# A long-convolution layer and a linear-memory attention layer in one kernel: two PSUM banks per product, Q's feature map in one piece, the last projection in five banks, a new written-out order

## The chip, the cores and the metric

The kernel runs on one core of a Trainium2 chip. The core has a matrix engine (TensorE, PE in the profile; its weight loads are PEld), a vector engine (VectorE, DVE), a scalar engine (ScalarE, ACT), GpSimd (POOL) and a queue engine (SyncE, SP) that here does nothing but issue transfers. Matrix products land in PSUM, eight banks of 512 fp32 columns on 128 partitions; DVE and ACT read them out into SBUF. The metric is the device time of one execution in microseconds; less is better. Three runs of the kernel before gave 274.84, 274.92 and 275.57 us.

## The reference

Two independent layers share the output, 640 columns each. With S = 2048 positions and D = 640 channels:

```python
# layer A: short causal filter on k, gate with v, long causal convolution, gate with q
kv = k_shift * v                                  # k_shift: 4 taps per channel
y = irfft(rfft(pad(kv)) * rfft(pad(ssm_k)))[:S]   # length 2S, per channel
a = q * (y + kv * ssm_D)

# layer B: 32 heads of 20, four segments of 512 positions
phi = lambda t: where(t > 0, t + 1.0, exp(t))
for s in range(4):
    p = softmax(qs @ ks.T * scale + mask)         # causal, inside the segment
    a_mem = (phi(qs) @ M) / (phi(qs) @ z + 1e-6)  # memory of earlier segments
    o = g * a_mem + (1 - g) * (p @ vs)
    M, z = M + phi(ks).T @ vs, z + phi(ks).sum()
b = concat(o) @ wo
return concatenate([a, b], axis=-1)
```

## The kernel before

**Layer A** (`conv`, line 428) runs over five slices `dp` of 128 channels. For each slice: the convolution's filter is brought in with positions on partitions (`load_filter`, 437; for slice 0 on PE as four groups `kt`, else by transposing transfers through DRAM); k is loaded transposed; the short filter is four PE groups `ks`, each one bank of 512 columns, and DVE multiplies each by v in place in `vt` (512). `spectrum` (515) transforms `vt` (X) and the filter (K) in eight PE groups F of 512 columns, read out by `evict` into a buffer F, followed by sums and differences on DVE (`B`). `product` (548) multiplies the spectra in sixteen DVE operations (`P1` to `YB`). `inverse` (584) goes back in four groups `I` of 512 columns, each multiplied by q on DVE into `qd` (597), and stores them; slice 4 stores each quarter on its own.

**Layer B** has eight units u: four segments s, each in two halves of 16 heads. `project` (636) takes four tiles of 128 positions: K, Q and V are three PE groups of 320 columns (`P`, `V`), read out by `evict`; K and Q of a tile are transposed by one transfer on SP into KQT (667). The feature map phi (668 to 680) is made for K in one piece of four tiles, and for Q in two pieces of two tiles; a piece is one exponential on ACT, two operations on DVE, and for Q a transposing transfer on SP into PqT. It is made for K in segments 0 to 2 and for Q in segments 1 to 3. Then comes an upper bound for the softmax (`kam`, `bound`: absolute values `qabs` of the transposed Q on DVE, a PE group `bd`, its read-out bT, four small `rows` transfers on SP into KQT). `attend` (722) makes ten times two blocks of scores on PE, each pair of banks read by one exponential of 1024 columns on ACT into a buffer ET, and then the values (`O`) with the memory's part in a second bank, a reciprocal and two products on DVE (`N`). `project_out` (815) transposes o (segments 0 to 2 by transfers on SP, segment 3 on PE as five groups `ot`) and multiplies it by wo: per segment four tiles, each two groups of 320 columns, and one store per tile. In segment 3 each group's matmuls are issued in three parts, by the channels of o that they need.

**What sets the order.** All operations are recorded first (`Recorder`, 105), each with the engine's queue that it goes to; a matmul group recorded under `rec.one()` is one operation, or one part of it. `ORDER` (866) is a packed list, a permutation of all operations, in which they are then issued (`issue`, 247; each instruction of the program carries line 256). Each engine works off its own share of that list strictly in that order, and so does SP with the transfers. `BASE` (889) gives each PSUM group its first bank. `EVICT` (863) has one digit per read-out: 1 sends it to DVE, 0 to ACT (`evict`, 387). Nothing is decided while the kernel runs. The first twenty PE groups (`warm`) multiply zeros while the first transfers come in.

The names in the profile are those of the buffers: `ET<-ps` is an exponential of scores, `F<-ps` the read-out of a spectrum, `KQ<-ps` and `Va<-ps` read-outs of K, Q, V, `vt<-ps,vt` the product of the short filter, `pq<-ps,pq` that of the inverse, `outb<-ps` and (in the last segment, where PP serves as a buffer) `PP<-ps` the read-outs of the last projection, `KQT<-KQ` and `PqT<-PP` the transposing transfers, `xT<-in_B_x` x's.

Of the kernel before, what the change touches and what calls it, by code (L numbers as in the profile page):

```python
# [16 lines left out]
ALU = mybir.AluOpType  # L17
# [4 lines left out]
S = 2048; D = 640  # L22
# [242 lines left out]
class Layer:  # L265
# [162 lines left out]
    def conv(self, dp):  # L428
# [31 lines left out]
        def short_filter():  # L460
# [33 lines left out]
            for b in range(4):  # L494
                key("ks", b)
                g = self.group(1, "ks")
                ps = g.ap[:, 0, :]
# [14 lines left out]
                V.tensor_tensor(out=vt[:, b], in0=ps.rearrange("p (c d) -> p c d", d=128), in1=vt[:, b], op=ALU.mult, grp=g)  # L512
# [71 lines left out]
        def inverse(U):  # L584
# [51 lines left out]
    def project(self, u):  # L636
# [5 lines left out]
        for t in range(4):  # L642
            tok = slice(128 * t, 128 * t + 128)
            rec.key = ("P", u, t)
            for i0 in range(0, 2, KQW):
                g = self.group(KQW, "kq")
                for i in range(KQW):
                    with rec.one():
                        for cc in range(5):
                            nc.tensor.matmul(g.ap[:, i, 0:320], lhsT=xT[:, cc, tok], rhs=self.wqkv[:, cc, half, i0 + i, :], start=(cc == 0), stop=(cc == 4), grp=g)  # L650
                self.evict(KQ[:, t, i0:i0 + KQW, :, 0:DH], g.ap[:, :, 0:320].rearrange("p i (h d) -> p i h d", d=DH), g)
            rec.key = ("V", u, t)
            g = self.group(1, "v")
            with rec.one():
                for cc in range(5):
                    nc.tensor.matmul(g.ap[:, 0, 0:320], lhsT=xT[:, cc, tok], rhs=self.wqkv[:, cc, half, 2, :], start=(cc == 0), stop=(cc == 4), grp=g)
            self.evict(Va[:, t, :, 0:DH], g.ap[:, 0, 0:320].rearrange("p (h d) -> p h d", d=DH), g)
# [10 lines left out]
            for i, n in ((0, 4), (1, 2)):  # L668
# [146 lines left out]
    def project_out(self, s):  # L815
# [13 lines left out]
        else:  # L829
            oTv = self.ring("xT", None)[:].rearrange("p c q -> p (c q)").rearrange("p (t c q) -> p t c q", t=4, c=5)  # L830
            for t in range(0, 4, 2):
                rec.key = ("oT", s, t)
                nc.sync.dma_start_transpose(out=oTv[:, t:t + 2].rearrange("p t c q -> p (t c) q"), in_=self.o_s[s][:, t:t + 2])
        for t in range(4):
# [32 lines left out]
c-jrrgMttW5Czb=cV=>JwrjI(+um&3wry{=YqM?Jwr#$5KH?;hgpx=SOA<*c$t1Z1N(ymFDKR9bq>|JUAo(PXq?L4%UNVSCM#(S5rG&(nOj1M&N>M2#1thZ+l7x&T#UzwOl)_R{vPd?GD$yjTv=&M_Ru  # L867
o89mX@*-N1{t2Mv-!&Vp2)cGmt4+Mq){M36cs@RjNxireH0}!<rIV^0I}rlxosSYDjI##|%ux29lBaS%3|tvec1!l9;)qoph2aQdc@ieJRM$5?k6xRtYPOq`f3zW692(>@3OIQQAr&c9R^;#a_}>nn)M
vA=xDh2T5~jCVeC~3$vf3W>?7}xuv_LWf2aRb<$e~$W-=~o)XM35>EO{JQ*lOS&TzuIE!<wWa1c(U|yNV5=_dmoW;pZ!`U3l;j&svaSn&c6lP{JR^W6FV;K&WJTgKmu_7yT97}TsOLC-yNEMEfF*2T2x
kkoHZI<OG87D7Um*u!omdkiq$So4Ytul!dqz*@N0XNHfnJA-KiyNdS=Q5m*mTEjCqqvCkSe-{ib&}NJVQIqfI+HtOmo(*kHsfM8=M;%6dt|q?py@uDEJtOk?3H?K%l%TGD<p>Ql<+cL>NAWsV0#8jJI2  # L870
(8T*7Xgz($-S0Xj{Va;AjUmh8?0a!`7(F}KM?u96wDjLW%FRx+A)W^~;yj<A?5D>zHKa0BCNS3*~@6+?JT;^|zWu4Ws?*VgR7dD4+<*`EU#Swo`}7t09=hvRZVF3Cv=g(#Xpd$JdANfO=2Q*uu3$Yn{Y
YdDan<)WOI-VBdq+J}R9L)Nh`T?2I!Bk664s&}OyZ^{x0gE)Fc&d7c)l;j#pugO(8z!Z9rgPBU#^SUgO)H;L-br0uDB2A-b<(@2%`|?2cavOW=KJMT{+05;Xj6S+dq9CnC(8uyfw(ufD>sF@I2<WTbG_
gj+C0=Gf-N}eLOuK7T9O7<9!f@Ti6FkYoTq;i`gQnC$dX7hUl;@dVfm1xqCz4Scg9t!0Twr`;(q}SQk1;x)%W-Db1ZavE5(7<ei!pJBu{5iW*DQL5u`ohk%59!yY`wx)l3gcgHqD`NahGpoq+a7yc2UJ
WUT0EF*Vl5NH`!GmGdAAJ5KV|1d@oP<MV>Ma9`GR(p&9aNGQ>jxO^kPvUmx)qCu)Cv&Lk+PA7y|VKFAAxma*Crlk}4m)=`>U$LVP8p;Ps%{F1zy96j}$<kUi%M~iC<{FYvt675hz15rx9OKEM7AM#VmX
h|)ilXZ%wKsvl)Q7x;}G!vSmnC3w_&47xU9vP7unUPDMXeFJYsZd$-Vx|t%@;X#=V76A#Y{-IKsGvD9Mzf=;25VL{*4$`?CR$DB=yGkKt<h8)X+xc>f7LCN{nNTyPgiI@%+m$h2J>~H#<Kiqi&<I#X|P
D^YdEW+1yNJ~$Y1GzAdPL2Ervyq`Y422`dgz|OnbwBQeD-SX(B6(@U~bxqK>A8;3JEo0cxw+TdvkW8p%HK9h>PAU8`%f4~ihbB3N^6p~cWrY46z=ZFQZt(gYUIT5EB%)A-h2*XsuDXx)&|x}$@3vJh?a
f43bqv6aL|?WCKu6GmBB>w*$UV%rqf8KZ5dMzvB{s@ruRB3ftNrO|D-Ho^{#W_xtACbQBQfUZbx4Y60ZXb;<u&wR~+2(+HIPs^a2ZPnwN+74)U`@*C)*izU@J*Z`ILWfvNJET2O73EP5?d`1g#9{4V=d
# [87 lines left out]
```

## Time and profile before

| | us |
|---|---|
| three runs, median | 274.92 |
| the profiled execution | 274.51 |
| its span, first to last instruction | 272.7 |
| PE busy | 259.2 |
| DVE busy | 252.3 |
| ACT busy | 244.4 |
| POOL busy | 6.9 |

The busy time of an engine is the time in which at least one of its instructions was under way; neighbouring instructions overlap, so the durations in a group's row add up to more. The clock of TensorE was granted in full throughout. A group's row shows engine, operation, output and inputs, shapes, count, then busy time and mean ns of one, then the idle time of the engine just before them with what ended it. In the timeline the columns are start, length, engine, and the operation; `x3` are three in a row. SPq marks the issuing of a transfer on SP. Matmul ends are modelled, and PE's busy time takes in waits between them.

### The profile page before, as it was taken

To read this page: it belongs to the slowest core of one execution; us is meant where nothing else is said; L and a number is where in the kernel's file an instruction comes from. 1 tells how busy PE (TensorE), PEld (TensorE's weight loads), DVE (VectorE), ACT (ScalarE), POOL (GpSimd) and SP (SyncE) were. 2 spreads that over 40 slices of the span, in tenths; PEclk is the share of its full clock that TensorE was granted. 3 is DMA by queue.
4 is the path that set the end of the run, shared out by engine and by line. 5 is a ranking of instruction groups with operands and counts; after the bars stand their busy time and mean duration, and the time that the engine had idled before them with its cause. 6 is when DMAs were issued, how large, how long until landed. Compare 5 with 4: busy or idle time off the path is not lost.

```text
span 272.7 us, 10081 instructions
## 1 busy us (share of the span) xinstructions
PE 259.2 (95%) x4337; PEld 193.8 (71%) x4339; DVE 252.3 (93%) x426; ACT 244.4 (90%) x378; POOL 6.9 (3%) x18
## 2 busy tenths in 40 slices
PE   8999999999999999869999999999999999898994
PEld 3888677768678678747777687777776876675883
DVE  0799999999999999969999999999998999999972
ACT  1374699999999999969999999999999999999953
POOL 9000000000000000000000000000000000000000
PEclk9999999999999999999999999999999999999999
DMA  6999889999779899997999899873996047581333
GB/s 202 296 240 175 203 184 193 262 233 176 138 160 167 192 223 169 119 249 173 174 160 211 186 223 148 172 118 79 157 182 152 29 84 146 122 138 45 64 105 118
DMA packets 131196, 44.79 MB, mean 164 GB/s; under 512 B 121563, under 2 KB 128736, under 8 KB 131024
## 3 DMA queue, kind: packets, MB, share of 16 engines
q1 hardware_dynamic: 130992, 43.96, 82.0%
q8 instruction: 34, 0.56, 0.9%
q0 software_dynamic: 160, 0.20, 0.2%
q14 instruction: 10, 0.08, 0.2%
HBM read 14.12 MB, written 7.34 MB: 79 GB/s over the span
## 4 chain that ended last, share of the span: by engine, by line
PE 53%; ACT 24%; DVE 11%; issue 4%; DMA 4%; SPq 3%; DVEq 0%; ACTq 0%
PE ps L256 53%; ACT ET L256 16%; ACT F L256 4%; SPq L256 3%; DVE pq L256 2%; ACT KQ L256 2%; DMA out_dram<-pq 2%; DVE Y L256 2%; DMA out_dram<-outb 1%; DVE o L256 1%; ACT Va L256 1%; ACT PP L256 1%; DVE Xh L256 1%; DVE Kh L256 1%; DVE F L256 1%
## 5 line engine op out<-in xcount | busy, mean ns | idle before, releaser
L256 ACT ACTIVATE ET<-ps 128x1024 bf16<-128x1024 f32 x160 | 159.0, 1072 | 0.9 <-PE ps L256 0.6
L256 PEld LDWEIGHTS <-xT 128*128 128x128 bf16 x640 | 58.8, 98 | 28.2 <-issue 6.5
L256 PE MATMUL ps<-wqkv,xT 128*128 128x320 bf16 x480 | 76.9, 299 | 1.9 <-DMA xT<-in_B_x_dram 1.0
L256 PE MATMUL ps<-Va,ET 128*128 128x21 bf16 x1280 | 42.8, 172 | 1.0 <-ACT KQ L256 0.6
L256 PEld LDWEIGHTS <-ET 128*128 128x128 bf16 x1280 | 40.0, 96 | 3.6 <-issue 2.4
L256 ACT CAST F<-ps 128x512 bf16<-128x512 f32 x71 | 39.8, 644 | 1.4 <-PE ps L256 1.4
L256 PE MATMUL ps<-KQT 32*128 32x128 bf16 (+2 forms) x896 | 35.2, 239 | 0.8 <-ACT ET L256 0.4
L256 PEld LDWEIGHTS <-Wf 128*128 128x128 bf16 x320 | 28.8, 97 | 5.8 <-issue 1.7
L256 ACT CAST KQ<-ps 128x320 bf16<-128x320 f32 x61 | 27.1, 477 | 5.9 <-PE ps L256 5.9
L256 PE MATMUL ps<-wo,xT 128*128 128x320 bf16 x160 | 25.8, 299 | 0.6 <-ACT ET L256 0.5
L256 PEld LDWEIGHTS <-KQT 32*128 32x128 bf16 x896 | 16.2, 92 | 11.3 <-issue 10.4
L256 PE MATMUL ps<-vt,Wf 128*128 128x256 bf16 x160 | 22.1, 273 | 0.3 <-ACT ET L256 0.3
L256 PE MATMUL ps<-kT,Wf 128*128 128x256 bf16 x160 | 21.3, 272 | 0.0
L256 PE MATMUL ps<-Y,Wi 128*128 128x256 bf16 x160 | 20.5, 273 | 0.2
L256 DVE TENSOR_TENSOR o<-ps,rr 128x640 bf16<-128x640 f32 x24 | 19.5, 812 | 0.2
L256 PE MATMUL ps<-Mbd,PqT 128*128 128x84 bf16 x96 | 18.4, 202 | 0.9 <-ACT ET L256 0.9
L256 DVE TENSOR_TENSOR Y<-Y,pq 128x2048 bf16<-128x2048 bf16 (+1 forms) x20 | 18.7, 935 | 0.0
L256 ACT ACTIVATE PP<-KQ 128x640 bf16<-128x640 bf16 (+1 forms) x18 | 17.5, 971 | 0.8 <-DVE KQ L256 0.7
L256 DVE TENSOR_TENSOR pq<-Xh,Kh 128x2048 bf16<-128x2048 bf16 x15 | 18.2, 1211 | 0.0
L256 PEld LDWEIGHTS <-Wi 128*128 128x128 bf16 x160 | 14.8, 98 | 3.4 <-issue 1.3
L256 PE MATMUL ps<-skd,kr 128*128 128x128 bf16 (+4 forms) x114 | 16.0, 255 | 0.4 <-ACT ET L256 0.3
L256 PEld LDWEIGHTS <-kr 128*128 128x128 bf16 x116 | 14.5, 148 | 2.3 <-issue 0.6
(90 smaller groups left out, 355.8 us busy)
## 6 DMA issues: line engine op xcount, KB each, us to landing
vt<-in_A_v_dram SPq DMA_DIRECT2D x10, 256.0 KB
pq<-in_A_q_dram SPq DMA_DIRECT2D x10, 256.0 KB
out_dram<-outb SPq DMA_DIRECT2D x13, 160.0 KB
turned<-kT SPq DMA_DIRECT2D x4, 512.0 KB
kT<-turned SPq DMA_DIRECT2D x8, 256.0 KB
out_dram<-pq SPq DMA_DIRECT2D x8, 256.0 KB
kb<-kr SPq DMA_DIRECT2D x6, 256.0 KB
Wf<-c_wf SPq DMA_DIRECT2D x4, 256.0 KB
```

The source lines that it names most:

```text
L256: f(*[fix(a) for a in args], **{k: fix(v) for k, v in kw.items()})
```

## The change

- **Two banks per operation in layer A.** Two neighbouring groups of the short filter (`KSW = 2`) take two banks side by side, and one DVE operation of 1024 columns multiplies both by v. The same for the inverse and q (`IW = 2`). The matmuls are the same. Slice 4's stores are issued in two sets of four.
- **Q's feature map in one piece** (`QN = 4`): four tiles at once: one exponential, two DVE operations and one transfer per unit in place of two each.
- **The last projection in five banks** (`WP = 1`): in segment 3, each of the four tiles has one group of 512 columns; the remaining 128 columns of the four tiles share a fifth group. Five read-outs of 512 columns in place of eight of 320, and five stores: four of 128 rows of 1024 bytes, one of 512 rows of 256 bytes.
- **A new order, new banks, new shares**: `ORDER` and `BASE` are replaced, and `EVICT` has 227 digits with 31 ones in place of 230 with 33. The program has 1476 operations in place of 1531, and 180 transfers on SP in place of 185.
- A joint group for K, Q and V is written but not used (`KQV = 0`).

```diff
-                g = self.group(1, "ks")
-                ps = g.ap[:, 0, :]
+                if b % KSW == 0:
+                    g = self.group(KSW, "ks")
+                ps = g.ap[:, b % KSW, :]
...
-                V.tensor_tensor(out=vt[:, b], in0=ps.rearrange("p (c d) -> p c d", d=128), in1=vt[:, b], op=ALU.mult, grp=g)
+                if b % KSW == KSW - 1:
+                    some = vt[:, b + 1 - KSW:b + 1].rearrange("p b c d -> p b (c d)")
+                    V.tensor_tensor(out=some, in0=g.ap, in1=some, op=ALU.mult, grp=g)
...
-                g = self.group(1, "I")
-                pyv = g.ap[:, 0, :].rearrange("p (a h d) -> p a h d", a=2, h=2)
+                if c % IW == 0:
+                    g = self.group(IW, "I")
+                pyv = g.ap[:, c % IW, :].rearrange("p (a h d) -> p a h d", a=2, h=2)
...
-                V.tensor_tensor(out=qd[:, :, c, :], in0=g.ap[:, 0, :].rearrange("p (b d) -> p b d", d=128), in1=qd[:, :, c, :], op=ALU.mult, grp=g)
+                if c % IW < IW - 1:
+                    continue
+                some = qd[:, :, c + 1 - IW:c + 1, :]
+                V.tensor_tensor(out=some, in0=g.ap.rearrange("p c (b d) -> p b c d", d=128), in1=some, op=ALU.mult, grp=g)
...
-                        nc.sync.dma_start(out=rows.rearrange("(p h c) d -> p c h d", h=2, c=4)[:, c], in_=qd[:, 2 * a:2 * a + 2, c, :])
+                        for n in range(c + 1 - IW, c + 1):
+                            nc.sync.dma_start(out=rows.rearrange("(p h c) d -> p c h d", h=2, c=4)[:, n], in_=qd[:, 2 * a:2 * a + 2, n, :])
...
-            for i, n in ((0, 4), (1, 2)):
+            for i, n in ((0, 4), (1, QN)):
...
+        if last and WP:
+            rem = self.group(1, "w")
+            rest = self.ring("outb", [128, 2, 320], n=2)[:].rearrange("p i j -> p (i j)")[:, 0:512]
+            for t in range(4):
+                g = self.group(1, "w")
+                for part in ((0, 1, 2), (3,), (4,)):
+                    with rec.one():
+                        for cc in part:
+                            nc.tensor.matmul(g.ap[:, 0, :], lhsT=oTv[:, t, cc, :], rhs=self.wo[:, cc, 0:512], start=(cc == 0), stop=(cc == 4), grp=g)
+                self.evict(spare[:, 512 * t:512 * t + 512], g.ap[:, 0, :], g)
+                nc.sync.dma_start(out=self.out[L * s + 128 * t:L * s + 128 * t + 128, D:D + 512], in_=spare[:, 512 * t:512 * t + 512])
...
+            for part in ((0, 1, 2), (3,), (4,)):
+                with rec.one():
+                    for t in range(4):
+                        for cc in part:
+                            nc.tensor.matmul(rem.ap[:, 0, 128 * t:128 * t + 128], lhsT=oTv[:, t, cc, :], rhs=self.wo[:, cc, 512:640], start=(cc == 0 and t == 0), stop=(cc == 4), grp=rem, skip_group_check=True)
+            self.evict(rest, rem.ap[:, 0, :], rem)
+            nc.sync.dma_start(out=self.out[L * s:L * s + 512, D + 512:2 * D].rearrange("(t p) j -> p t j", p=128), in_=rest.rearrange("p (t j) -> p t j", t=4))
+            return
...
+WP = 1
+KSW, IW = 2, 2
+KQV, QN = 0, 4
...
-EVICT = ("01011011111000100000001000000000000000000000000000000000000001000000000000001010000000101100000100000000000000000001000000000000000000000000"
-         "000000000100001110000000000000000000000000010001000000000000010100100000100001010001100100")
+EVICT = ("01010010000000010000001000000000000000000000000000000000000000000000000000000000000000011000110100100000000000000000001100000000000000000000"
+         "000000000010111010000000100000000100000000100001001001010000000100100000110100000000100")
```

More of the change, by code (lines that the diff above doesn't have):

```diff
@@ L644, in project @@
             rec.key = ("P", u, t)
-            for i0 in range(0, 2, KQW):
-                g = self.group(KQW, "kq")
-                for i in range(KQW):
+            if KQV:
+                g = self.group(2, "kqv")
+                w = self.wqkv[:, :, half].rearrange("p c i j -> p c (i j)")
+                for b in range(2):
                     with rec.one():
                         for cc in range(5):
-                            nc.tensor.matmul(g.ap[:, i, 0:320], lhsT=xT[:, cc, tok], rhs=self.wqkv[:, cc, half, i0 + i, :], start=(cc == 0), stop=(cc == 4), grp=g)
-                self.evict(KQ[:, t, i0:i0 + KQW, :, 0:DH], g.ap[:, :, 0:320].rearrange("p i (h d) -> p i h d", d=DH), g)
@@ L652, in project @@
[L652 to L657, printed above, removed]
+                            n = 512 - 64 * b
+                            nc.tensor.matmul(g.ap[:, b, 0:n], lhsT=xT[:, cc, tok], rhs=w[:, cc, 512 * b:512 * b + n], start=(cc == 0), stop=(cc == 4), grp=g)
```

68 lines of the change are left out of this document (44 added, 24 removed).

## The prediction, made before the result was known

> **What bounds the kernel now.** I read the page's totals first, then the busy times in stretches of 10 us, then the chain, then the timeline of the places where the engines stop.
>
> ```profile
> span 272.7 us, 10081 instructions
> PE 259.2 (95%) x4337; PEld 193.8 (71%) x4339; DVE 252.3 (93%) x426; ACT 244.4 (90%) x378; POOL 6.9 (3%) x18
> ```
> The profiled execution took 274.51 us: 1.8 lie around the span, and it is 0.41 under the median of 274.92. In the stretches the columns are window, length, and busy us of PE, PEld, DVE, ACT, POOL (instructions in brackets).
>
> ```profile
> 0.00:10.00 10.00, 8.74 (x61) 4.75 (x62) 2.87 (x6) 2.37 (x4) 6.86 (x18) 1.00 0.80 238
> 10.00:20.00 10.00, 9.95 (x92) 8.51 (x91) 9.05 (x17) 6.31 (x13) 0.00 (x0) 1.00 1.05 250
> 20.00:30.00 10.00, 10.00 (x87) 7.88 (x86) 10.00 (x20) 4.91 (x10) 0.00 (x0) 1.00 1.06 210
> 30.00:40.00 10.00, 9.70 (x143) 7.26 (x141) 9.97 (x14) 8.61 (x18) 0.00 (x0) 1.00 0.84 171
> 50.00:60.00 10.00, 9.72 (x158) 6.90 (x154) 10.00 (x18) 10.00 (x18) 0.00 (x0) 1.00 0.99 254
> 110.00:120.00 10.00, 7.76 (x145) 5.93 (x142) 7.45 (x16) 8.67 (x14) 0.00 (x0) 1.00 1.08 162
> 260.00:273.00 13.00, 9.22 (x144) 7.19 (x142) 6.16 (x13) 5.35 (x10) 0.00 (x0) 1.00 0.38 115
> ```
> ACT and DVE together are the limit: both are full from 40 us to the tail, apart from a hole at 110 to 120. Only the first 40 us, where ACT idles 17.8 us while DVE is full from 20 on, the hole, and the tail have room. PE's busy share overstates it, since the ends of matmuls are modelled.
>
> **The two places where time stands still.** First the start: chain, then PE and DVE in the timeline.
>
> ```profile
> 35.04 1.85 ACT ET L256 x2
> ```
> ```profile
> 29.01 0.40 PE L256 MATMUL ps<-qabs,A 128*32 128x512 bf16 x4
> 29.34 4.93 PE L256 MATMUL ps<-wqkv,xT 128*128 128x320 bf16 x35
> 34.20 0.40 PE L256 MATMUL ps<-KQT 32*128 32x384 bf16 x8
> ```
> ```profile
> 27.86 0.68 DVE L256 TENSOR_SCALAR qabs<-KQT 128x2048 int16<-128x2048 int16 x1
> ```
> The first exponentials (ET) come at 35 us because DVE reaches qabs of unit 0 only at 27.86, the bound's matmuls follow at 29.01, and seven projection groups (35 matmuls, 0.70 us a group) stand ahead of the first scores. Then the hole, on SP and on DVE:
>
> ```profile
> 106.78 5.62 SPq L256 DMA_TRANSPOSE xT<-in_B_x_dram  x1
> ...
> 113.80 1.96 SPq L256 DMA_TRANSPOSE PqT<-PP  x1
> 115.80 1.31 SPq L256 DMA_TRANSPOSE KQT<-KQ  x1
> ```
> ```profile
> 119.39 0.69 DVE L256 TENSOR_SCALAR qabs<-KQT 128x2048 int16<-128x2048 int16 x1 [2.55 <-issue]
> ```
> DVE stands 2.55 us for unit 3's last KQT transposition, issued at 115.80 behind x's transposition and one of Q's map on the SP queue.
>
> **The change, part by part.** Durations of one operation (mean ns after the comma):
>
> ```profile
> L256 ACT ACTIVATE ET<-ps 128x1024 bf16<-128x1024 f32 x160 | 159.0, 1072 | 0.9 <-PE ps L256 0.6
> L256 ACT CAST F<-ps 128x512 bf16<-128x512 f32 x71 | 39.8, 644 | 1.4 <-PE ps L256 1.4
> L256 DVE TENSOR_TENSOR pq<-ps,pq 128x512 bf16<-128x512 f32 x20 | 13.7, 684 | 0.7 <-PE ps L256 0.2
> L256 DVE TENSOR_TENSOR o<-ps,rr 128x640 bf16<-128x640 f32 x24 | 19.5, 812 | 0.2
> L256 ACT ACTIVATE PP<-KQ 128x640 bf16<-128x640 bf16 x12 | 9.6, 798 | 0.0
> L256 ACT ACTIVATE PP<-KQ 128x1280 bf16<-128x1280 bf16 x6 | 7.9, 1315 | 0.8 <-DVE KQ L256 0.7
> L256 DVE TENSOR_TENSOR PP<-PP,qabs 128x640 bf16<-128x640 bf16 x12 | 5.8, 483 | 0.2 <-ACT F L256 0.2
> L256 DVE TENSOR_TENSOR PP<-PP,qabs 128x1280 bf16<-128x1280 bf16 x6 | 4.9, 816 | 0.0
> L256 DVE TENSOR_SCALAR qabs<-KQ 128x640 bf16<-128x640 bf16 x12 | 3.7, 306 | 0.0
> L256 DVE TENSOR_SCALAR qabs<-KQ 128x1280 bf16<-128x1280 bf16 x6 | 2.9, 475 | 0.0
> ```
> Neighbours overlap, so what an operation costs its queue is the spacing of starts:
>
> ```profile
> 11.90 1.29 DVE L256 CAST kT<-ps 128x512 bf16<-128x512 f32 x2 [0.88 <-PE ps L256]
> 13.11 0.48 DVE L256 CAST KQ<-ps 128x320 bf16<-128x320 f32 x1
> 16.28 0.78 ACT L256 CAST KQ<-ps 128x320 bf16<-128x320 f32 x2
> 17.79 0.59 ACT L256 CAST F<-ps 128x512 bf16<-128x512 f32 x1 [0.25 <-PE ps L256]
> 18.47 0.43 ACT L256 CAST KQ<-ps 128x320 bf16<-128x320 f32 x1
> 256.62 5.61 ACT L256 ACTIVATE ET<-ps 128x1024 bf16<-128x1024 f32 x6
> ```
> On DVE two of 512 take 1.29, one 0.69, so one costs 0.60, an overlap of about 0.08; one of 320 costs 0.48 - 0.08 = 0.40. On ACT (5.61 - 1.07)/5 = 0.91 for 1024 columns, 0.78 - 0.43 = 0.35 for 320, and about 0.47 for 512 (0.91 less 512 columns at (0.91 - 0.35)/704 = 0.8 ns is 0.50; F's 0.59 less ET's overlap of 0.16 is 0.43).
>
> *Two banks per operation* (short filter and inverse): 40 DVE products of 512 become 20 of 1024. One of 1024 is not in the trace from PSUM. 640 against 512 gives (812 - 684)/128 = 1.0 ns a column, so it costs 0.60 + 0.53 = 1.13: 0.07 saved per pair, 1.4 us on DVE. Bounds: 0 if the fixed part doubles, and 0.15 per pair (durations without overlap), 3.1 us. [...]
>
> *Q's map in one piece*: for the six units with a map, two sets of 640 become one of 1280. ACT: 2 x 798 - 1315 = 281 ns less one overlap of 0.16, 0.12 a unit, 0.7 us in all. DVE: (2 x 306 - 475) + (2 x 483 - 816) less two overlaps of 0.08 = 0.13 a unit, 0.8 in all. Twelve transpositions become six of twice the size: SP's time per byte I leave as it is. PqT is complete later, but only O's first matmuls read it, behind a whole group's exponentials; without that cover a unit would wait for one half more, 1.3 to 2.0 us (rows above).
>
> *Evictions*: the list of 0 and 1 counted against the code. DVE (0.60 for 512, 0.40 for 320): F 9 to 4, KQ 3 to 8, Va 2 to 4, projection 10 to 9 small and 1 large, bT 1 to 2, kT 3 to 1, oT 2 to 0, xT 3 to 2 (0.73 each): -2.5 us. ACT (0.47 and 0.35): F 71 to 76, KQ 61 to 56, Va 30 to 28, projection 22 to 15 small and 4 large, bT 7 to 6, kT 1 to 3, oT 3 to 5, xT 1 to 2: +1.3. So DVE's work falls by 1.4 + 0.8 + 2.5 = 4.7 us, ACT's changes by 1.3 - 0.7 = +0.6. ACT is now the bound, and what counts is where it stands idle.
>
> *The order.* Unpacked, the strings of the diff are permutations of the code's operations, which can be counted per queue.
> Start: ahead of qabs of unit 0 DVE has 36 operations now and 32 after (the memset at the start aside): F 4 to 2, kT 3 to 1, xT 3 to 2, KQ 2 to 4, 4 products to 2 double ones, one small one more: -1.2 - 1.2 - 0.7 + 0.8 - 0.1 + 0.1 = -2.3 us. ACT takes these in its idle time; it has 36 operations ahead of the first exponential both times. Between the bound's matmuls and the first scores stand five projection groups in place of seven, -1.4 us. Against it, the 512 KB filter load moves ahead of x and wk; at the 238 to 250 GB/s of the first two windows that is 2.1 us during which PE makes the filter's transposes, which it otherwise makes later. I take -2.0 for the first exponential (bounds: -3.7 both gains, +1.5 the load not made good).
> Between first and last exponential ACT's own list gives +0.6, less the evictions that moved ahead of the first (F +2, kT +2, xT +1, KQ -4, Va -1: 0.9 + 0.9 + 0.6 - 1.4 - 0.35 = +0.7) and those that moved behind the last (5 small and 2 of 512 become 7 of 512: 3.3 - 2.7 = +0.6): 0.6 - 0.7 - 0.6 = -0.7 us.
> The hole: the last KQT transposition of unit 3 still stands behind x's, but ahead of it on SP three transpositions of Q's map have become one of twice the size, one of o has moved behind, and the load of wo has moved ahead: two times 1.3 to 2.0 us less against one short issue. DVE, 4.7 us lighter, also reaches a unit's bound earlier. I take -0.9 for all holes, a third of this one; bounds -2.5 (this one gone) and +5 (two more like it).
> Tail:
>
> ```profile
> 262.20 0.36 DVE L256 RECIPROCAL rr<-ps 128x32 f32<-128x32 f32 x1 [1.04 <-PE ps L256]
> 265.66 3.56 PE L256 MATMUL ps<-wo,xT 128*128 128x320 bf16 x25
> 265.86 0.59 ACT L256 CAST xT<-ps 128x512 bf16<-128x512 f32 x1 [0.92 <-PE ps L256]
> 269.25 0.43 ACT L256 CAST PP<-ps 128x320 bf16<-128x320 f32 x1 [0.47 <-PE ps L256]
> 269.70 0.33 SPq L256 DMA_DIRECT2D out_dram<-PP  x1
> ```
> 25 matmuls of 320 take 3.56, 0.14 each, after the last transpose of o. The new order leaves 16 of 512 (0.22 by columns) and 4 of 128 (0.06) there: 3.7. The last eviction is 0.47 to 0.59 in place of 0.43, but the last three small DVE operations start about 0.4 earlier, since the second-last group no longer waits behind the last exponentials. The segment's stores become five short issues in place of four, all but the last behind other work. I take 0 (bounds -0.5 and +1.0).
> Sum: -2.0 - 0.7 - 0.9 + 0 = -3.6: 274.51 - 3.6 = 270.9 for a profiled execution, 271.3 against the median.
>
> **The rivals.** *Slower: Q's one transposition blocks SP.* It stands directly ahead of rows of units 3 and 7, and of a KQT transposition of unit 4. Each is twice the 1.31 to 1.96 above, so 1.3 to 2.0 more at once; x's row shows that 5.62 can come of a busy DMA. Three such delays of 2.55, as at 119.39, are 7.6 us: 274.92 - 3.6 + 7.6 = 278.9; it decides from 3.6 us, two delays (276.4). SP's unbroken issuing from 106 to 117 speaks for it; against it, rows wait for the bound anyway. 0.21.
> *The start gives nothing*: the filter load first, x 2.1 us later, and only the gaps shrink: 274.92 - 1.6 = 273.3. 0.15.
> *Banks instead of operations*: a two-bank group keeps its first bank until all 1024 columns are read, 0.53 us longer, and DVE begins only after the second bank. With 20 such groups and a third of them on PE's path, 3.5 us come back: 274.8, the same. [...] In the trace PE's longest kind of wait for banks is short (columns: us in total, times, longest), so 0.12.
>
> ```profile
> PE ps L256 <- ACT ET L256: 3.2, 11, 0.5
> ```
> *More than forecast*: first exponential at -3.7 and the hole gone: 274.92 - 3.7 - 0.7 - 2.5 = 268.0. 0.07.
>
> **How the numbers follow.** The forecast has 0.45, with a range of its own of 269.7 to 272.9. 0.3% (0.8 us) is about what a measurement can tell from none. Faster: 0.45 + 0.15 + 0.07 + 0.02 of the banks' case = 0.69; same: 0.08 of it; slower: 0.21 + 0.02 = 0.23. 268.0 to 276.4 leaves out the dearer half of the first rival and what lies beyond both.
>
> **What would show it.** DVE near 248 us busy, ACT near 245; products of 1024 at about 1.21 us; first exponentials near 33 us; a DVE gap ahead of unit 3's qabs well under 2.55; last eviction near 266. Wrong it is if new gaps ahead of qabs or exponentials add up to over 3.6 us, or if the first exponential stays at 35.

## The result: 1.1% slower

The changed kernel took 277.57 us (median of four runs, 276.76 to 278.80) beside 274.88 for the kernel before: a ratio of 1.0114, 95% interval 1.0070 to 1.0157. Measured a second time, it gave 1.0107 (1.0060 to 1.0154). The forecast was 271.3 us, with a range that ended at 276.4. The profiled execution took 276.82 us, its span is 275.0. In all ratios, runs more than 1.5% above the fastest run of their kernel are left out as slow: six of twelve for one kernel below (the row's move), three at most for any other, so the table of the experiments gives the ratio of the medians of all runs beside them.

First the engines' totals, from the page of the changed kernel, then two of its groups. They answer to the rows of the prediction in which the exponentials have 0.9 us of idle time ahead of them and the products come in forms of 512.

```profile
PE 259.9 (94%) x4339; PEld 193.9 (70%) x4339; DVE 248.6 (90%) x392; ACT 245.8 (89%) x371; POOL 7.0 (3%) x18
...
L256 ACT ACTIVATE ET<-ps 128x1024 bf16<-128x1024 f32 x160 | 159.8, 1090 | 6.7 <-PE ps L256 6.5
```
```profile
L256 DVE TENSOR_TENSOR vt<-ps,vt 128x1024 bf16<-128x1024 f32 x10 | 12.2, 1223 | 1.6 <-PE ps L256 1.0 <-issue 0.5
L256 DVE TENSOR_TENSOR pq<-ps,pq 128x1024 bf16<-128x1024 f32 x10 | 12.2, 1220 | 1.7 <-ACT ET L256 1.5
```

The work came out as computed: DVE 248.6 us (248 was said), ACT 245.8 (245), a product of 1024 columns 1.22 us (1.21). What went wrong shows in one column: the idle time ahead of the exponentials grew from 0.9 to 6.7 us, nearly all of it waiting for PE.

Two places make up 4.4 us of it (waits of 1.26, 0.32 and 2.85). These are lines of the changed kernel's timeline (start, length, engine, operation, idle time before with what ended it) around the first, with SP's issues that belong to it:

```profile
30.97 0.68 SPq L256 DMA_DIRECT2D KQT<-bT  x1
31.70 0.57 SPq L256 DMA_DIRECT2D vt<-in_A_v_dram  x1
...
32.32 2.58 SPq L256 DMA_TRANSPOSE kr<-in_A_k_dram  x1
...
34.23 1.02 ACT L256 ACTIVATE ET<-ps 128x1024 bf16<-128x1024 f32 x1 [0.53 <-PE ps L256]
34.94 2.08 SPq L256 DMA_TRANSPOSE kT<-in_A_ssm_k_dram  x1
...
37.07 1.16 SPq L256 DMA_DIRECT2D KQT<-bT  x2
...
41.63 0.40 PE L256 MATMUL ps<-KQT 32*128 32x384 bf16 x8 [1.52 <-DMA KQT<-bT]
42.06 1.94 ACT L256 ACTIVATE ET<-ps 128x1024 bf16<-128x1024 f32 x2 [1.26 <-PE ps L256]
...
44.31 1.02 ACT L256 ACTIVATE ET<-ps 128x1024 bf16<-128x1024 f32 x1 [0.32 <-PE ps L256]
```

The first of unit 0's four rows is issued at 30.97. The second, which the scores S.0.1.A need, stands behind a load of v and two transpositions and is issued at 37.07; the matmuls that wait for it start at 41.63. The second place is the one on which the prediction spent most words, around unit 3's bound, but it is not qabs that waits:

```profile
115.42 1.02 ACT L256 ACTIVATE ET<-ps 128x1024 bf16<-128x1024 f32 x1
...
118.16 1.51 PE L256 MATMUL ps<-wqkv,xT 128*128 128x320 bf16 x5 [2.29 <-DMA xT<-in_B_x_dram]
...
120.21 0.69 DVE L256 TENSOR_REDUCE kam<-ps 128x4 f32<-128x512 f32 x1 [2.55 <-PE ps L256]
...
120.70 1.02 ACT L256 ACTIVATE ET<-ps 128x1024 bf16<-128x1024 f32 x1 [2.85 <-PE ps L256]
```
```profile
97.30 4.26 SPq L256 DMA_TRANSPOSE PqT<-PP  x1
...
102.31 2.73 SPq L256 DMA_TRANSPOSE KQT<-KQ  x1
...
107.06 2.63 SPq L256 DMA_TRANSPOSE KQT<-KQ  x2
...
110.54 4.21 SPq L256 DMA_TRANSPOSE xT<-in_B_x_dram  x1
```

PE's next operation is P.4.0, the first projection of unit 4, and it needs x, whose transposition was issued at 110.54 (106.78 before). Behind P.4.0 in PE's queue stand the groups that unit 3 and the exponentials need (kx of the bound, the scores S.2.2.A, memory 3). The first two could have run at about 117 us: in the run with P.4.0 behind them, below, they start at 116.91 and 117.23, and memory 3 at 118.38. So PE stood still for 2.29 us, and DVE and ACT ran out of work behind it. In the old order these groups stood ahead of the projection, which waited 0.99 for x.

A third thing lies in the same place. Cut into windows (length, busy time of PE, PEld, DVE, ACT, POOL, the granted clock, DMA share, GB/s):

```profile
114.00:116.00 2.00, 1.88 (x66) 1.44 (x63) 2.00 (x7) 1.86 (x4) 0.00 (x0) 1.00 1.08 237
116.00:118.00 2.00, 0.00 (x0) 0.00 (x0) 1.66 (x4) 1.85 (x3) 0.00 (x0) 0.96 1.20 104
118.00:120.00 2.00, 1.84 (x9) 1.10 (x9) 0.00 (x0) 0.00 (x0) 0.00 (x0) 0.50 1.13 228
120.00:122.00 2.00, 2.00 (x25) 1.19 (x25) 1.79 (x2) 1.30 (x2) 0.00 (x0) 0.69 0.84 181
122.00:124.00 2.00, 2.00 (x34) 1.41 (x31) 1.62 (x4) 2.00 (x5) 0.00 (x0) 1.00 1.21 245
```

From 117.82 to 121.24 us PE ran at half its clock (0.50 granted): P.4.0's five matmuls of 320 columns took 1.51 us in place of 0.84. The profile of before had no such stretch. In every profile of this case the changes of the clock lie whole multiples of 3.41 us apart; in this one, recorded from 5.18 us on, full, half and full clock last 112.64, 3.41 and 153.60 us, 33, 1 and 45 times 3.413. PE had been idle for 1.94 us when the clock fell here (115.88 to 117.82), and in the experiments for much less (0.52 of the 3.00 us from 222, in the changed kernel's second profile below).

The time adds up between the profiled executions. First exponential 34.91 to 34.23: -0.7. From there to the end of the last, 227.31 to 230.17 us, +2.9: ACT's busy time in that stretch 224.12 to 223.63, -0.5, and the rest, in which ACT is idle, 3.19 to 6.54, +3.35. Tail 10.5 to 10.6. Together +2.3, the difference of the spans.

### The profile page after: what moved, and what is told of

Same layout as the page of the kernel before. It is cut to its first block, busy times and chain, and to the rows that moved or that the text cites. A ratio compares the mean times of both kernels' runs of the same rounds, so it can differ in the third digit from the quotient of the medians.

```text
span 275.0 us, 10010 instructions
## 1 busy us (share of the span) xinstructions
PE 259.9 (94%) x4339; PEld 193.9 (70%) x4339; DVE 248.6 (90%) x392; ACT 245.8 (89%) x371; POOL 7.0 (3%) x18
## 4 chain that ended last, share of the span: by engine, by line
PE 44%; ACT 29%; DVE 13%; issue 6%; DMA 4%; SPq 2%; DVEq 0%; ACTq 0%
PE ps L256 44%; ACT ET L256 21%; DMA xT<-in_B_x_dram 3%; DVE Xh L256 2%; ACT KQ L256 2%; ACT F L256 2%; SPq L256 2%; DVE Y L256 2%; DMA KQT<-bT 2%; DVE Kh L256 2%; DVE o L256 1%; DVE F L256 1%; DVE vt L256 1%; DVE qabs L256 1%; ACT PP L256 1%
## 5 line engine op out<-in xcount | busy, mean ns | idle before, releaser
L256 PEld LDWEIGHTS <-xT 128*128 128x128 bf16 x640 | 58.0, 98 | 31.4 <-issue 6.8
L256 ACT CAST F<-ps 128x512 bf16<-128x512 f32 x76 | 45.6, 673 | 5.8 <-PE ps L256 3.8
L256 PE MATMUL ps<-KQT 32*128 32x128 bf16 (+2 forms) x896 | 34.4, 240 | 1.5 <-DMA KQT<-bT 1.5
L256 ACT CAST KQ<-ps 128x320 bf16<-128x320 f32 x56 | 25.7, 510 | 1.6 <-PE ps L256 1.5
L256 PE MATMUL ps<-wo,xT 128*128 128x320 bf16 (+2 forms) x160 | 25.5, 299 | 0.4 <-ACT ET L256 0.4
L256 PE MATMUL ps<-kT,Wf 128*128 128x256 bf16 x160 | 22.1, 272 | 0.4 <-ACT ET L256 0.3
L256 ACT ACTIVATE PP<-KQ 128x1280 bf16<-128x1280 bf16 x12 | 16.5, 1375 | 0.0
L256 PE MATMUL ps<-pack 32*128 32x128 bf16 x512 | 14.2, 216 | 1.6 <-ACT ET L256 1.3
```

The source lines that it names most:

```text
L256: f(*[fix(a) for a in args], **{k: fix(v) for k, v in kw.items()})
```

## The experiments

The theory after the result: the new order puts two transfers on PE's path that the old one hid, and the gaps cost the clock on top. Rivals: the start, where the filter load stands ahead of x; the two-bank operations; Q's one transposition. Numbers of operations in the diffs are indices into the recorded list; a move changes the place of one operation in its engine's queue. "Stretches" are half-clock stretches per run, from each run's granted clock: (1 - clock) x 2 x time / 3.41, rounded to a whole number for each run (in the profiles, what is left over is a half clock in the last 2 us, behind PE's work), then the mean over the runs that the ratios compare. The kernel before has 0.4 in 84 runs, the changed one 1.7 in ten.

| | ratio to before | interval | medians of all runs | stretches | idle ahead of exponentials |
|---|---|---|---|---|---|
| changed kernel, again | 1.0107 | 1.0060 to 1.0154 | 1.0107 | 1.5 | 6.4 |
| P.4.0 later on PE | 1.0133 | 1.0078 to 1.0189 | 1.0127 | 1.4 | 3.8 |
| row earlier on SP | 1.0068 | 1.0021 to 1.0115 | 1.0134 | 1.2 | 8.2 |
| both | 1.0041 | 1.0008 to 1.0075 | 1.0056 | 1.6 | 4.3 |
| filler | 1.0077 | 1.0044 to 1.0110 | 1.0084 | 0.0 | 6.6 |
| both and filler | 1.0027 | 0.9989 to 1.0065 | 1.0020 | 0.1 | 3.0 |
| filler of 32 rows | 1.0060 | 1.0020 to 1.0099 | 1.0079 | 0.7 | 6.6 |
| one bank per operation | 1.0117 | 1.0074 to 1.0159 | 1.0127 | 1.5 | 6.7 |
| x first at the start | 1.0111 | 1.0063 to 1.0159 | 1.0142 | 1.8 | 6.9 |
| Q's map alone, old order | 1.0044 | 1.0015 to 1.0074 | 1.0050 | 0.3 | 2.1 |

(The last column is the profile's, of one execution each, from the row of the exponentials, in us.)

**The two gaps.**

> The changed kernel once more, as the measure for the runs beside it. If the loss is in the program and not in one chip's mood: again about 1.1% over the kernel before, near 277 us; two gaps in the exponentials, at 40 to 45 and at 116 to 121 us, and the granted clock at one half from about 118 to 121 us.

> In PE's order alone the projections of unit 4 (tiles 0 and 2) are moved two to three places back, behind the product kx of unit 3's bound, the scores S.2.2.A and memory 3; the transfers and all other engines keep their order. Theory of the misplaced wait: x's transposition lands near 118 us whatever PE does, but now only the projection waits for it. ACT's gap of 2.85 and DVE's of 2.55 us near 120 shrink below 0.7 each, PE's idle stretch falls under 1 us and the granted clock stays at 1.0 from 116 to 121 us; 2 to 3 us less than the changed kernel, about 274.3 to 275. Rival, the wait only moves: the projection of unit 4 is then what is late, and its K, Q and rows hold up unit 4's exponentials 20 us later by as much; time as the changed kernel, 277.

```diff
+    order.remove(992)
+    order.insert(order.index(907) + 1, 992)
+    order.remove(1006)
+    order.insert(order.index(992) + 1, 1006)
```

(992 and 1006 are the first groups of tiles 0 and 2 of unit 4, 907 is memory 3.)

> On SP alone the second of unit 0's four rows transfers is moved directly behind the first, ahead of the transposition of k (2.58 us of issuing) and of the filter (2.08 us) for slice 1. Theory of the late row: the row is issued near 31.5 in place of 37.07 and PE's wait of 1.52 us ahead of S.0.1.A goes, with ACT's 1.38 and 0.43 us; 1 to 1.8 us less than the changed kernel, about 275.5. Rival, the row is late but something else is as late: the matmuls of slice 1's short filter wait for k's transposition instead, and under 0.4 us comes back.

```diff
+    order.remove(563)
+    order.insert(order.index(562) + 1, 563)
```

(562 and 563 are the first two rows of unit 0.)

> Both moves together. If the two gaps are separate, their gains add: 3 to 4.5 us less than the changed kernel, 272.7 to 274, which is 0.3 to 0.8% faster than the kernel before. If the second gap is only hidden by the first (DVE or ACT is the bound behind it and takes the gain back), no more than the better one of the two: about 275.

The move on PE did at its place what was said. In the profile of that kernel:

```profile
117.65 0.68 DVE L256 TENSOR_REDUCE kam<-ps 128x4 f32<-128x512 f32 x1
...
119.57 1.67 PE L256 MATMUL ps<-wqkv,xT 128*128 128x320 bf16 x11 [0.39 <-DMA xT<-in_B_x_dram]
```

The reduction for unit 3's bound comes at 117.65 in place of 120.21 and the projection's wait is 0.39. Its profiled execution took 275.62 us, but the ratio over its runs shows no gain: with one gap still there and the clock falling 1.4 times a run, a single move can't be told from none. The row's move gave 0.4% by the ratio, inside the uncertainty, and nothing by the medians of all twelve runs (1.0134), though its profiled execution shows the first gap gone (rows issued together at 31.00). The same profile shows why one execution is not enough: in it x landed later still.

```profile
119.50 1.51 PE L256 MATMUL ps<-wqkv,xT 128*128 128x320 bf16 x5 [3.76 <-DMA xT<-in_B_x_dram]
...
122.04 1.94 ACT L256 ACTIVATE ET<-ps 128x1024 bf16<-128x1024 f32 x2 [4.32 <-PE ps L256]
```

PE's wait ahead of P.4.0, with the same order there on SP and PE, was 2.29 and 1.16 us in the two profiled executions of the changed kernel, 3.76 here, and 2.53 and 2.90 in those with one bank and with x first. Both moves together take the ratio from about 1.011 to 1.0041: 277.7 to 275.9 us on the mean, 1.8 of the 3.0 us lost (1.2 on the mean of all runs, 276.4).

**The clock.** In the changed kernel's second profile the clock fell where PE had hardly been idle:

```profile
222.00:225.00 3.00, 2.48 (x62) 1.72 (x61) 3.00 (x5) 3.00 (x5) 0.00 (x0) 1.00 1.04 171
225.00:228.00 3.00, 3.00 (x21) 2.07 (x18) 2.36 (x6) 1.93 (x3) 0.00 (x0) 0.54 0.83 159
```

So another count was made from the matmuls of all 18 traces: for each 3.41 us of the grid the sum of columns times rows out of 128, as a share of what fits at 2.4 columns per ns, as matmuls are spaced at full clock in these traces (512 columns follow each other in 216 ns, 320 in 135 or 136, which is 2.37). Scores have 32 rows, so a PE that is busy with scores counts for a quarter. Of the stretches that themselves ran at full clock, all 9 with a sum under 0.30 were followed by a half clock; of those from 0.32 to 0.37, 6 of 10; of the others none. Columns without the rows don't tell them apart: 0.94 was followed by a half clock in one profile, and 0.53 was not in that of before. Wherever the grid falls, the new order has three places that can come under 0.34, at 114 to 118, 222 to 226 and 248 to 252 us; the old order's lowest is 0.34, for a moment. Where the grid falls differs by execution (the clock falls at 117.82, 225.26 and 251.25 us of three profiles, the last with both moves: 1.8, 3.4 and 2.1 us past a multiple of 3.413), so a place costs the clock in some of them and not in others.

> The changed kernel with eleven matmuls more on PE whose results nobody reads (128 rows by 512 columns each, 0.21 us at full clock): six ahead of the projection P.4.0, two ahead of the scores S.6.0.A, three ahead of S.7.1.D; nothing else is changed. The profiles so far show half-clock stretches of exactly 3.41 us, all on one grid of 3.41 us, and each began after a stretch in which PE's matmuls, counted as columns times rows out of 128, filled less than about 0.36 of the time; the changed kernel has three such places (114 to 118, 222 to 226, 248 to 252 us), the kernel before has none. Theory of the clock: with the filler no place is under 0.4, the granted clock of nearly every run is 1.000 in place of 0.988 on the mean, and the time falls by 1.2 to 1.7 half-clock stretches at 1.2 us each, about 2 us less than the changed kernel: near 275.5. Rival, the clock only follows the waits and the time is set by the transfers: clock 1.000, but the time stays at 277.5. Second rival, what counts is an idle gap and not the work in the stretch: the clock still falls near 225 and 250 in some runs.

```diff
+FILL = ((6, 2, 992), (2, 0, 1280), (3, 0, 1395))
...
+    for count, bank, ahead in FILL:
+        rec.key = ("fill",)
+        fill = K.group(1, "fill")
+        base.append(bank)
+        with rec.one():
+            for n in range(count):
+                rec.nc.tensor.matmul(fill.ap[:, 0, :], lhsT=K.ident[:], rhs=K.Wf[:, 0, 0, :], start=True, stop=True, grp=fill)
+        order.insert(order.index(ahead), len(rec.ops) - 1)
```

> The changed kernel with the same eleven filler matmuls in the same places, but with 32 rows in place of 128; 512 columns each as before, results read by nobody. They keep PE just as busy in time. Theory that the clock goes by columns times rows: the filler adds a quarter as much, the places at 114 to 118 and 248 to 252 us stay under 0.36, and the mean number of half-clock stretches per run is nearer to the changed kernel's 1.5 to 1.7 than to the full filler's 0.08: over 0.7. Rival, PE's busy time counts: under 0.3 as with the full filler. The time is then 277 to 278 or 276.5.

```diff
+                rec.nc.tensor.matmul(fill.ap[:, 0, :], lhsT=K.ident[0:32, :], rhs=K.Wf[0:32, 0, 0, :], start=True, stop=True, grp=fill)
```

> The two moved waits (projection of unit 4 later on PE, second row of unit 0 earlier on SP) together with the filler (two matmuls ahead of P.4.0, two ahead of S.6.0.A, three ahead of S.7.1.D). The two moves alone gave 276.3 us with a clock of 0.99 on the mean. Theory of the clock: 1.000 in nearly all runs and 1.2 to 2 us less, 274.3 to 275, no slower than the kernel before. Rival, the clock is a consequence: 276.3 again.

Eleven useless matmuls took the stretches from 1.7 a run to none (one in all twelve runs), and the time from 1.011 to 1.0077 (0.9 us by the ratios); the gaps themselves stayed (6.6 us). The intervals of the two ratios overlap, and so do those of the same step with both moves made (1.0041 to 1.0027, with seven filler matmuls): both go the same way, but neither is clear of the noise. Within the kernels of this study, a run with one more stretch is 1.0 us longer (standard error 0.13, a slope over 206 runs; late transfers can cause both, so it is no pure price; the 1.2 us of what was expected was the author's estimate). That the half clock costs about 1 us is thus likely, and not shown by itself. The same matmuls with 32 rows left 0.7 stretches a run, at the mark that was set (0.67 rounded for each run, 0.78 not), against none: that PE is busy is not enough, rows count. The profile of that run has a half clock from 117.48, right behind six of them. In time the two fillers can't be told apart (1.0060 and 1.0077). Nor does PE's idle time tell the stretches apart: the half clock at 225.26 in the changed kernel's second profile came behind 0.52 us of it in 3.00, while in the profile of before the clock stayed whole behind 1.55 us of it in 3.41 (116.88 to 120.29).

With both moves and the filler the kernel can't be told from the one before: 1.0027 (0.9989 to 1.0065), 275.1 us on the mean. By the ratios, the three together account for about 2.2 of the 3.0 us lost, and the 0.3% that is left can't be told from none. How the 2.2 us divide among them is less sure than the sum.

**The code parts.**

> The changed kernel with every product of 1024 columns (short filter and q) done as two operations of 512 in the same place, same banks, same order. If two banks per operation are worth what their spacing says (1.20 against 1.13 us), DVE has 20 times 0.07, 1.4 us more to do, and the time is 0 to 1.4 us longer than the changed kernel's, 277.6 to 279. If holding the first bank longer and waiting for the second is what costs, the time falls by up to 3 us, towards 274.6.

```diff
-                    V.tensor_tensor(out=some, in0=g.ap, in1=some, op=ALU.mult, grp=g)
+                    with rec.one():
+                        for n in range(KSW):
+                            V.tensor_tensor(out=some[:, n], in0=g.ap[:, n], in1=some[:, n], op=ALU.mult, grp=g)
```

The inverse's product was split in the same way. DVE's busy time is 249.4 in place of 248.6, and the time is the same: 1.0117 against 1.0107 and 1.0114. Two banks per operation neither cost nor gave anything that can be measured. That DVE has slack there, while ACT and PE set the pace, would explain it; it was not tried apart. The banks' rival, in so far as it is about releasing the first bank sooner for DVE, falls with it; that the group keeps both banks for the next user was the same in both kernels and wasn't tried apart.

> The kernel before, in its own order and banks, with Q's feature map alone in one piece: one exponential, two DVE operations and one transposition of twice the size per unit, each at the place of the later one of the two it replaces (in unit 4 one of the DVE operations stands three places earlier). Theory of the order: the code part by itself costs nothing; 0.8 us less on DVE and 0.7 on ACT, so 0 to 1 us less than the kernel before, 273.5 to 274.6. Rival of the blocked queue: a transposition of 3 to 4 us at once holds up rows and transposes behind it and lands later itself, and the memory's part of the values waits for it: 1 us or more slower than the kernel before.

```diff
-            for i, n in ((0, 4), (1, 2)):
+            for i, n in ((0, 4), (1, 4)):
```

Alone, in the old order, Q's map in one piece is 0.44% slower (0.15 to 0.74), 1.2 us. The work that it was to take away hardly shows in the busy totals: DVE 252.1 us beside 252.3, ACT 244.4 both times. Its profile has one wait that the larger piece makes:

```profile
93.59 1.34 ACT L256 ACTIVATE PP<-KQ 128x1280 bf16<-128x1280 bf16 x1
...
96.22 0.25 PE L256 MATMUL ps<-Va,ET 128*128 128x21 bf16 x4 [1.16 <-ACT KQ L256]
```

The exponential of Q's map stands for 1.34 us at once in ACT's queue, the read-outs and score exponentials behind it come later, and PE waits 1.16 for them. The old order had two pieces of 0.80 in two places. But this wait isn't the loss in that execution: from the first exponential to the end of the last it took 227.4 us, beside 227.3 before. Of the 1.2 us between the two spans, 1.1 lie ahead of the first exponential (36.03 beside 34.91), where no map of Q is made yet. Over its runs the kernel is slower; the cause stays open.

**The start.**

> The start alone is put back: the 512 KB filter load is issued behind x and the first weights, as in the kernel before, and PE's transposes of the filter with their read-outs behind x's. Theory of the start: the first projection comes about 2 us sooner on PE (10.5 to about 8.5 us), unit 0's bound with it, and the first exponential falls from 34.2 to between 32.3 and 33.5 us; 0.7 to 2 us less than the changed kernel. Rival, the filter's spectrum is then late by as much and DVE's sums of slice 0 hold up the bound: the first exponential stays at 34 or comes later, time 277 to 279.

```diff
+    order.remove(72)
+    order.insert(order.index(5) + 1, 72)
...
+    base[7] = 3
```

(Also moved: PE's four transposes of the filter and two of their read-outs, behind x's.) The rival's outcome held: the time is that of the changed kernel, and the first exponential is no earlier.

```profile
10.21 2.20 PE L256 MATMUL ps<-wqkv,xT 128*128 128x320 bf16 x15
```
```profile
35.09 1.02 ACT L256 ACTIVATE ET<-ps 128x1024 bf16<-128x1024 f32 x1 [0.53 <-PE ps L256]
```

The first projection comes at 10.21; in the 15 profiled executions that have the changed start it comes at 9.97 to 11.34 and the first exponential at 33.74 to 35.06, and before they stood at 8.16 and 34.91. So the position of the filter load alone doesn't bring x forward (x's first transposes on PE start at 8.02 here, 8.08 in the changed kernel, 6.61 before). From the first projection to unit 0's qabs PE has next to no pause: it is busy 19.65 of 19.70 us before, 18.61 of 18.61 in the changed kernel, 19.66 of 19.71 here, and DVE 18.38, 15.10 and 15.71. That points to PE's queue and not to DVE as what sets the first exponential; no run tried it.

**What stands behind the late x.** Six kernels went on to the next waits. None came near 1.0027, and four of them show what SP's queue hides.

> The changed kernel with one move on SP: x's transposition for segment 2 is issued ahead of two KQT transpositions of unit 3 and one load of v (at about 107 in place of 110.5 us); PE's order is as in the changed kernel. Theory of the late transfer: x lands near 115 in place of 118 us, PE's idle time of 1.2 to 3.8 us ahead of P.4.0 goes, with ACT's 2.85 us; 1.5 to 3 us less than the changed kernel, 274.5 to 276. Rival: what x passes is then late, unit 3's KQT lands 4 us later, DVE's qabs of unit 3 waits instead, and nothing is won.

```diff
+    order.remove(969)
+    order.insert(order.index(872), 969)
```

1.0122 (1.0068 to 1.0176): nothing won. PE no longer waits for x, but for unit 3's first row:

```profile
119.94 3.10 SPq L256 DMA_TRANSPOSE kT<-in_A_ssm_k_dram  x1
121.20 0.69 DVE L256 TENSOR_SCALAR qabs<-KQT 128x2048 int16<-128x2048 int16 x1
123.09 0.59 SPq L256 DMA_DIRECT2D out_dram<-pq  x1
123.78 3.09 SPq L256 DMA_TRANSPOSE PqT<-PP  x1
127.06 0.60 SPq L256 DMA_DIRECT2D KQT<-bT  x1
...
130.39 0.40 PE L256 MATMUL ps<-KQT 32*128 32x384 bf16 x8 [2.54 <-DMA KQT<-bT]
```

The bound's qabs is 4.3 us earlier than in the changed kernel (121.20 against 125.46), and the row comes only 0.7 us earlier (127.06 against 127.80): ahead of it stand a filter's transposition and Q's, 3.1 us each. This is the place of the prediction's first rival. It is a second gap behind the first, not the one that made the kernel slow.

> x's transposition for segment 2 earlier on SP as in the run before (which gave 1.0122 of the kernel before and moved PE's idle time from P.4.0 to the scores of unit 3, 2.54 us for KQT<-bT), and with it Q's transposition of unit 3 and the filter's of slice 3 behind the first rows transfer of unit 3. Theory of the queue: the row was late since those two (3.09 and 3.10 us of issuing) stood ahead of it on SP; the row is issued near 123.5 in place of 127.06, PE's wait of 2.54 us goes, and the time falls by 1.5 to 3 us against the run before, 275 to 277.5 with the first gap and the clock still in it. Rival: Q's map or the filter is then late for the values of unit 3 or the spectrum, and the wait only moves once more: 278 to 279.

```diff
+    order.remove(893)
+    order.insert(order.index(903) + 1, 893)
+    order.remove(338)
+    order.insert(order.index(893) + 1, 338)
```

1.0217 (1.0169 to 1.0266): slower still. The row was issued at 125.60, only 1.5 us earlier, since the read-out that it carries (bT) ended at 125.58; SP stood empty for it, and everything behind it was late:

```profile
120.09 1.36 SPq L256 DMA_DIRECT2D out_dram<-pq  x2
...
125.60 0.59 SPq L256 DMA_DIRECT2D KQT<-bT  x1
126.25 3.14 SPq L256 DMA_TRANSPOSE PqT<-PP  x1
129.43 2.08 SPq L256 DMA_TRANSPOSE kT<-in_A_ssm_k_dram  x1
131.56 1.62 SPq L256 DMA_TRANSPOSE xT<-o_s  x1
...
135.34 1.51 PE L256 MATMUL ps<-wo,xT 128*128 128x320 bf16 x5 [4.63 <-DMA xT<-o_s]
```

From 121.45 to 125.60 SP issued nothing; then the transposition of o is issued at 131.56, and PE stands 4.63 us for it. The two transpositions had filled just this hole. So Q's transposition ahead of the row is not the fault that the rival made of it: with Q's and the filter's behind the row, the kernel is slower.

> The two moved waits and the filler (that kernel gave 1.0027 of the kernel before), and with them the first row of unit 3 ahead of Q's and the filter's transpositions on SP, and the scores S.0.1.A ahead of the short filter's first two groups of slice 1 on PE (which waited 0.86 us for k). If these were the next waits: 0.5 to 1.5 us less, 273.5 to 274.5 beside 274.9 for the kernel before. If the short filter or the filter's spectrum is late then: the same or slower, 275 to 276.

> As the run beside it, and x's transposition for segment 2 earlier on SP too. With the row of unit 3 out of the way it takes 0.5 to 1.5 us more off, 272.5 to 274; if unit 3's KQT transpositions, which x passes, are what is late, it is 1 us or more slower than the run beside it.

Both had the two transpositions behind the row (the second also x's earlier) and were 2.3 and 2.8% slower than the kernel before, with the same wait for o (4.8 and 4.1 us on PE).

> The two moved waits and the filler, and in four places a score group is put between two PE groups that the changed order has back to back (the two groups of one two-bank product, 1.9 us together): S.0.0.J ahead of A.1.ks.3, S.4.0.J ahead of A.4.ks.1, S.4.1.A ahead of A.2.I.3, S.6.1.A ahead of A.3.I.3. In the profile of the kernel with moves and filler the exponentials wait 0.3 to 0.5 us at each of these places. Theory: 0.3 us less at each, 1 to 1.5 us in all, 273.3 to 274 and so no slower than the kernel before. Rival: the scores find no free banks there (ACT still holds them), and the wait stays: 274.8.

> The same, and x's transposition for segment 2 earlier on SP too. If x is still what unit 4 waits for, another 0.5 to 1 us less: 272.5 to 273.5, faster than the kernel before. If unit 3's KQT transpositions, which x passes, are now late, it is 0.5 to 2 us slower than the same kernel without the move.

1.0089 (1.0054 to 1.0123) and 1.0217 (1.0162 to 1.0271). The scores put between two neighbouring groups started earlier, and the next ones later: the waits in the first of the two grew to 0.73 and 1.01 us just behind the moves, ahead of the exponentials at 46.11 and 230.97. In the second the wait for unit 3's first row is back (2.32 us on PE). No version that beats both kernels was found.

## Why the prediction was wrong

**The holes: the step that failed.** The prediction took "-0.9 for all holes, a third of this one", with bounds of -2.5 and +5. ACT's idle time between the first exponential and the end of the last grew by 3.35 us in the profiled execution. The bound held; the value had the wrong sign. The prediction's own sign of being wrong came true too: the idle time ahead of the exponentials grew by 5.8 us (6.7 from 0.9), over the 3.6 that it named. The term was read from the one hole of before (qabs at 119.39) and from what stands ahead of its KQT on SP, and that hole is in fact gone:

```profile
125.46 0.68 DVE L256 TENSOR_SCALAR qabs<-KQT 128x2048 int16<-128x2048 int16 x1
```

But the step looked at one wait that the old order had, not at the transfers that the new order puts behind others: the second row of unit 0 behind two transpositions (1.5 us), and x behind Q's and three of KQT, with PE's groups arranged so that ready ones wait behind the one that needs x (2.3 us). Which operation stands behind which can be read from the order before any run: where PE's queue has an operation that needs a transfer, what is behind it? How long the wait is can't: x's differed by 2.6 us between executions.

**The clock: not a term at all.** The prediction has no term for it, and its rows of before show the clock granted in full. 1.3 stretches more per run came with the new order; the filler, which takes them away, made the kernel 0.9 us faster by itself and 0.4 us on top of both moves, which is not clear of the noise, and the slope over the runs gives 1.0 us for each stretch.

**The start: mis-sized.** -2.0 forecast, -0.7 measured. It has three parts. The first projection came 2.4 us later (10.53 in place of 8.16); the sum had priced the filter load ahead of x at 2.1 and taken it as made good, and it was not. From there to unit 0's qabs 19.70 us became 18.61, -1.1, where -2.3 was forecast from DVE's operations: DVE's busy time ahead of qabs did fall by 2.0 (19.78 to 17.79), but PE was busy all the while, as above. From qabs to the first exponential 7.05 became 5.09, -1.96, where -1.4 stood. The load's place is not all of it: with x first nothing was gained. And a single pair of executions is weak here: the changed kernel's second one has its first exponential at 34.96, and the kernel with Q's map alone, whose start is the old one, at 36.03.

**Right in size, without worth.** DVE's work (-3.7 on the page where -4.7 was summed, at 248 as said), ACT's own work in the span of the exponentials (-0.5 against -0.7), the product's price (1.13 said; starts of 126.07 and 127.20 on DVE give 1.13, though the prediction's 1.0 ns a column gives 0.51 and not 0.53 for 512) and the tail (+0.1 against 0). Of DVE's 4.7 us the product's part was undone by itself, and that changed nothing in the time; the other parts were not.

**The rivals.** Q's one transposition blocking SP (0.21) was the right kind of cause, a full SP queue, at the wrong place: three late bounds were forecast, and it was x and a row of unit 0. At unit 3 the place showed itself only when x had been moved. Q's map alone made the old order slower too, for a cause that stays open. "The start gives nothing" (0.15) had the late x right; the first exponential still came 0.7 earlier in the profiled execution. Banks (0.12) found no support.

**Where the expected gain went.** With the three causes gone (both moves and filler) the profiled span is 272.2 beside 272.7, and the 0.5 us are the start's (first exponential 0.9 earlier). From there to the end of the last exponential it is 227.5 beside 227.3: ACT's work is 0.2 less, its idle time 0.4 more (3.55 beside 3.19). The old hole is gone, but 3.0 us of idle time stand ahead of exponentials where 0.9 stood, most of it in waits of 0.3 to 0.5 us at 41, 43, 170, 172 and 226 us. The first follows PE's wait of 0.86 for k, whose transfer now goes behind the row. The others stand behind pairs of groups of one two-bank product, which PE does back to back: in this profile

```profile
170.18 1.92 PE L256 MATMUL ps<-Y,Wi 128*128 128x256 bf16 x16
...
172.53 1.02 ACT L256 ACTIVATE ET<-ps 128x1024 bf16<-128x1024 f32 x1 [0.30 <-PE ps L256]
```

That the pairing causes these waits is argued from their place; the two kernels that parted the pairs were slower, so it is not shown.

## What to carry to other kernels

In a kernel whose order is fixed, price a new order by its queues: for each operation that needs a transfer, find when SP can issue that transfer, and what ready work stands behind the operation. Work saved on an engine that doesn't set the pace at that place may be worth nothing: 0.8 us of DVE's was put back here and the time stayed. Larger operations are not sure to help in an order made for smaller ones. Compare several executions before a wait is named as the cause: the wait for one transfer differed by 2.6 us between executions with the same order there. Look at the granted clock of many runs, not of one profile: here a stretch with little matmul work, counted with its rows, cost PE half its clock in some executions and not in others (1.7 half-clock stretches a run, 0.4 in the kernel before).

## What was unexpected of the hardware

In these traces the half clock comes in stretches of 3.41 us (at times two on end, 6.83) on a grid whose place differs by execution, and it goes by columns times rows (under 0.30 of the full rate it followed 9 times of 9, over 0.37 never) and not by PE's busy time: six times it was halved with PE busy for 69 to 85% of the 3.41 us before, largely with scores of 32 rows, while it stayed whole behind stretches with 50 to 56%. Eleven matmuls of 128 rows (eleven times 216 ns, 2.4 us of PE) kept it whole in eleven of twelve runs, where the same eleven with 32 rows left 0.7 half-clock stretches a run. The same transposition of x, issued at the same place of the queue, made PE wait 1.16 to 3.76 us in five executions of kernels with the same order there.
